# Turning one norm by DMA, moving two feed-forward blocks forward, and letting VectorE take shared-port work

## The chip, the cores and the metric

The kernel runs on one core of a Trainium2 chip. A core has five engines that run side by side: TensorE (PE in the profile, with its weight loads as PEld), VectorE (DVE), ScalarE (ACT), GpSimd (POOL) and SyncE (SP), whose queue issues all DMA transfers here. The metric is the device time of one execution in microseconds, as a median over runs.

## The reference

One transformer block over 2048 rows of 512 features, with shifts, scales and gates from a condition vector `c`:

```python
mod = (_silu(c) @ w_mod).reshape(c.shape[0], 6, 1, -1)
sa, ca, ga, sb, cb, gb = (mod[:, i] for i in range(6))
h = _layernorm(x) * (1 + ca) + sa
x = x + ga * A(h)     # attention: 32 heads of 128, the last 512 rows of the k and v caches
h = _layernorm(x) * (1 + cb) + sb
x = x + gb * B(h)     # (gelu(h @ w_gate) * (h @ w_up)) @ w_down, inner size 1376
```

## The kernel before

Numbers that go through PE are kept as two fp16 parts, a high one and a low one; a product is three matmuls (high with high, high with low, low with high). Making the two parts is a constant need: ACT copies to the high part (`nc.scalar.activation(..., AF.Copy)`), and a subtraction makes the low part. The helper `tt` writes such a subtraction or sum once, as an operation that POOL or DVE may do.

**Stages.** An opening computes the condition's products, norms the rows and prepares the first heads. The attention stage makes 128 steps, each one head for one block of 512 rows (`slot`): query product, scores, exponentials, DMA transposes of the probabilities, product with v, product with wo, added to `acc`. From head pair `WINO` on, query products of four steps are shared by a seven-product scheme over 2 x 2 blocks (`w_product`; sums of inputs go through POOL). While it runs, the largest absolute value of each weight tile is found (`h_max`, four tiles side by side in `mx`); once for each head pair and kind, `h_send` writes the 128 x 4 maxima to DRAM, and `spread_max` reads them back to every partition, reduces them and makes the scale and its inverse.

The feed-forward stage works on two pairs of row blocks: pair 0 is rows 0 to 1023, pair 1 the rest. A unit `(p, f)` is pair p with column block f of 128 of the inner size. It uses the same seven products (`product`), for which the weight parts of block f are made once (`aw_make`: scaling, four sums, six splits) and, for some blocks, shared by both pairs. `UNITS` is the order of the units, `SPLIT` those that make their own parts, `MAKE` which parts are made ahead of which unit. The norm of the second pair (row blocks 2 and 3) hangs on units (0, 2) and (0, 3) of that list through `P1`; its sums on unit (0, 4).

The second norm of one row block is: statistics (`ln2_stats`), four tiles normed in fp32 (`ln2_norm`), four chunks, each turned by four fp32 transposes on PE into a PSUM bank and then scaled and shifted (`ln2_chunk`), and its high and low parts (`ln2_high`, `ln2_low`).

**What sets the order.** Nothing is issued as written. Class `Weaver` records every operation with its cost and dependences, plays the program several times with priorities worked back from the end, and issues what it found; its `Port` is why nearly every row of the profile has line L444. Its costs for each engine stand in `cost`. An operation may be recorded for two engines (`either`), and `sooner` decides in the play which takes it: the one that would end first. POOL and an operation on DVE that reads two SBUF tensors are marked `lock`: the play never lets them overlap. In `sooner`, such an operation on DVE is charged `SHY`, 1500 ns, on top of its cost. Where POOL follows DVE closely, `issue` makes POOL wait for that DVE operation. Any change in the program draws the whole order anew.

## Time and profile before

| | |
|---|---|
| Median of 3 runs | 1657.21 us (1657.04 to 1657.3) |
| Profiled execution | 1657.58 us, its span 1655.8 us |
| Mean granted PE clock | 0.997 |
| Busy: PE, DVE, ACT, POOL | 1642.4, 1289.3, 1216.6, 1305.0 us |
| Matmuls | 7732 |
| DMA | 228.61 MB, 138 GB/s on average |

Busy time is the union of an engine's instructions. For PE the ends are modelled: an instruction's duration includes its way out of the array, while the next one may already have started, so a pace is read from starts. In a row of a timeline, a name such as `psQ<-ident,T` gives the tile that is written and those that are read: `ps...` are PSUM banks, `psS` scores, `pp` probabilities in two parts, `st` row statistics, `raw` loaded weights, `top`, `iv` and `av` a crossing's maximum, scale and inverse, `aw` weight parts of the feed-forward stage, `hid` its inner activations, and `B`, `T` block inputs in two parts.

### The profile page before, as it was taken

How to read it: one execution, taken by the hardware profiler on the slowest of the kernel's cores; microseconds unless marked ns; L12 is line 12 of the kernel's file. 1: busy time of each engine (PE TensorE's matmuls, PEld its weight loads, DVE VectorE, ACT ScalarE, POOL GpSimd, SP SyncE). 2: the span in 40 equal slices, each digit the busy share in tenths (PEclk: the TensorE clock that was granted, in tenths of full speed). 3: DMA queues.
4: the chain of work that ended last, by engine and by line, in shares of the span. 5: the costliest groups of instructions: out<-in, count | busy, mean ns of one | idle time of the engine just before them, and what ended most of it. 6: DMA issues, size and time to landing. Idle time of an engine off the chain costs nothing.

```text
span 1655.8 us, 24293 instructions
## 1 busy us (share of the span) xinstructions
PE 1642.4 (99%) x7732; PEld 764.5 (46%) x7732; DVE 1289.3 (78%) x2381; ACT 1216.6 (73%) x2418; POOL 1305.0 (79%) x1097
## 2 busy tenths in 40 slices
PE   8999999999999999999999999999999999999999
PEld 4444444444444444444444444444444444444455
DVE  7777787878787788788999887888887956656557
ACT  5987797777787777888778777787878876545451
POOL 5999986868586878787768889999977898784682
PEclk9999999999999999999999999999999999999999
DMA  7676697878787778999999997788877712101111
GB/s 241 128 144 130 135 157 143 152 138 149 144 143 140 153 136 157 186 196 194 196 200 205 189 167 148 147 175 179 168 129 158 144 28 64 42 25 51 42 45 52
DMA packets 686289, 228.61 MB, mean 138 GB/s; under 512 B 596432, under 2 KB 663056, under 8 KB 686160
## 3 DMA queue, kind: packets, MB, share of 16 engines
q1 hardware_dynamic: 686160, 227.05, 69.1%
q8 instruction: 61, 1.00, 0.3%
q14 instruction: 68, 0.56, 0.1%
HBM read 78.98 MB, written 5.38 MB: 51 GB/s over the span
## 4 chain that ended last, share of the span: by engine, by line
PE 91%; ACT 2%; POOL 2%; DVE 2%; DMA 1%; SPq 1%; issue 1%; DVEq 0%; POOLq 0%; ACTq 0%
PE psS L444 31%; PE psW L444 23%; PE psO L444 21%; PE psQ L444 17%; SPq L444 1%; DVE st L444 1%; DVE acc L444 1%; DMA pT<-pp 1%; ACT p L444 0%; POOL pp L444 0%; POOL B L444 0%; DMA wm<-in_w_mod_dram 0%; POOL aw L444 0%; ACT T L444 0%; DMA raw<-in_B_w_up_dram 0%
## 5 line engine op out<-in xcount | busy, mean ns | idle before, releaser
L444 POOL TENSOR_TENSOR pp<-p,pp 128x1024 f16<-128x1024 f32 x256 | 545.9, 2132 | 212.8 <-ACT pp L444 97.3
L444 ACT ACTIVATE p<-psS,st,es 128x512 f32<-128x512 f32 x512 | 393.4, 774 | 187.7 <-DVE st L444 186.8
L444 DVE SCALAR_TENSOR_TENSOR acc<-psW,st,acc 128x512 f32<-128x512 f32 x496 | 367.2, 742 | 79.8 <-PE psW L444 77.7
L444 PE MATMUL psW<-wo,oT 128*128 128x512 f16 x1536 | 416.3, 379 | 0.0
L444 PE MATMUL psS<-kT,q 128*128 128x512 f16 x1536 | 379.1, 379 | 2.0 <-ACT q L444 2.0
L444 PE MATMUL psO<-pT,v 128*128 128x512 f16 x1536 | 377.1, 379 | 0.3 <-DMA pT<-pp 0.2
L444 DVE TENSOR_REDUCE st<-psS 128x2 f32<-128x1024 f32 x256 | 312.5, 1221 | 60.0 <-PE psS L444 59.6
L444 ACT ACTIVATE pp<-p 128x1024 f16<-128x1024 f32 x256 | 271.0, 1059 | 3.7
L444 PEld LDWEIGHTS <-q 128*128 128x128 f16 x1536 | 149.9, 98 | 182.1 <-ACT q L444 2.6
L444 PEld LDWEIGHTS <-v 128*128 128x128 f16 x1536 | 150.0, 98 | 181.3 <-DMA pT<-pp 1.2
L444 PEld LDWEIGHTS <-oT 128*128 128x128 f16 x1536 | 150.2, 98 | 180.1 <-DVE oT L444 0.5
L444 PEld LDWEIGHTS <-aw 128*128 128x128 f16 (+1 forms) x840 | 84.2, 100 | 95.1 <-issue 2.0
L444 ACT ACTIVATE oT<-psO 128x512 f16<-128x512 f32 x128 | 76.1, 594 | 66.2 <-PE psO L444 66.1
L444 PE MATMUL psQ<-T,S 128*128 128x512 f16 x504 | 123.3, 379 | 0.0
L444 PE MATMUL psQ<-B,A 128*128 128x512 f16 x480 | 119.6, 381 | 0.1
L444 PE MATMUL psS<-T,aw 128*128 128x512 f16 (+1 forms) x480 | 116.9, 379 | 0.0
L444 DVE SCALAR_TENSOR_TENSOR oT<-psO,oT 128x512 f16<-128x512 f32 x128 | 88.0, 688 | 30.9 <-ACT oT L444 30.6
L444 PEld LDWEIGHTS <-A 128*128 128x128 f16 x696 | 68.3, 98 | 83.3 <-issue 2.3
L444 PEld LDWEIGHTS <-S 128*128 128x128 f16 x672 | 65.8, 98 | 79.3
L444 ACT ACTIVATION_READ_ACCUMULATOR p<-psS,st,es 128x1 f32 x512 | 101.0, 197 | 0.0
L444 POOL TENSOR_TENSOR q<-h,q 128x512 f16<-128x512 f32 x84 | 97.5, 1161 | 2.0 <-ACT q L444 1.8
L444 DVE TENSOR_REDUCE mx<-raw 128x1 f32<-128x512 f32 x128 | 84.2, 674 | 15.6 <-DMA raw<-in_A_wq_dram 9.1
(211 smaller groups left out, 2295.6 us busy)
## 6 DMA issues: line engine op xcount, KB each, us to landing
raw<-in_A_k_cache_dram SPq DMA_DIRECT2D x32, 256.0 KB, 3.9
raw<-in_A_wq_dram SPq DMA_DIRECT2D x32, 256.0 KB, 3.7
raw<-in_A_v_cache_dram SPq DMA_DIRECT2D x32, 256.0 KB, 3.3
raw<-in_A_wo_dram SPq DMA_DIRECT2D x32, 256.0 KB, 3.2
pT<-pp SPq DMA_TRANSPOSE x512, 3.3
sa<-most SPq DMA_DIRECT2D x29, 256.0 KB, 3.8
raw<-in_B_w_gate_dram SPq DMA_DIRECT2D x24, 256.0 KB, 3.1
raw<-in_B_w_up_dram SPq DMA_DIRECT2D x24, 256.0 KB, 3.4
```

The costliest lines, as they stand in the source:

```text
L444: made[n] = real(*a, **k)
```

## The change

There are four edits.

1. The charge `SHY` on a DVE operation that shares POOL's port holds only for operations recorded before `calm`. `calm` is set where the feed-forward code begins in the text; at that point only the opening has been recorded, because the attention stage's operations are recorded by the loop over `slot` further below.
2. The second norm of row blocks 2 and 3 is turned by DMA. `turned_norm` norms a tile with a scale of `HS` folded in, splits it into high and low fp16 parts, `turned` sends both through DMA transposes, and `turned_chunk` joins them again with scale and shift in two operations (one more on DVE). The 32 fp32 transposes on PE go.
3. Units (0, 8) and (0, 9) come ahead of the second pair's first unit, which is now (1, 8); blocks 8 and 9 share weight parts between the pairs, and (1, 6) and (1, 7) make their own, so `SPLIT` has 18 units for 16.
4. In a crossing the maxima are written to DRAM by kind, so that the reduction reads neighbours; the scaling after it moves from DVE to POOL.

```diff
-            mine = max(t, shared[e] if kinds[e][1] else 0.0) + kinds[e][0] + (e == "DVE" and kinds[e][1]) * self.SHY
+            mine = ... + (e == "DVE" and kinds[e][1]) * (self.SHY if n < self.calm else 0.0)
...
+            if big:
+                nc.gpsimd.tensor_scalar(RS[key], RS[key], HS, 1.0, op0=OP.mult, op1=OP.mult)
...
-        t = DG[which[0]] = dram.tile([P, 4], F32, name="most", tag="most", bufs=3)
-        nc.sync.dma_start(t, m[:, 0:4])
+        t = DG[which[0]] = dram.tile([4, P], F32, name="most", tag="most", bufs=3)
+        nc.sync.dma_start(t.rearrange("a p -> p a"), m[:, 0:4])
...
-        nc.vector.tensor_reduce(r, w.rearrange("p (k a) -> p a k", a=4), op=OP.max, axis=AX.X)
+        nc.vector.tensor_reduce(r, w.rearrange("p (a k) -> p a k", a=4), op=OP.max, axis=AX.X)
...
-        nc.vector.tensor_scalar(iv[:, 0:4], r, 1e-30, ROUND / top, op0=OP.max, op1=OP.mult)
+        nc.gpsimd.tensor_scalar(iv[:, 0:4], r, 1e-30, ROUND / top, op0=OP.max, op1=OP.mult)
...
+    nc.calm = len(nc.ops)
...
+    TURNED = (2, 3)
+
+    def turned_norm(qg, j):
+        if j % 2 == 0:
+            t = b_tile(0, N2TAG[qg][j // 2], (P, 2, 2, 2, N // 2))
+            N2[qg, j], N2[qg, j + 1] = t[:, 0], t[:, 1]
+            RT["norm"] = right.tile([P, 2, N], F32, name="hf", tag="p32", bufs=2)
+        n, t = RT["norm"][:, j % 2, :], N2[qg, j]
+        nc.either((S_, V), lambda o: ln_norm(("2", qg), n, acc[4 * qg + j], j, o))
+        n = n.rearrange("p (a n) -> p a n", a=2)
+        nc.scalar.activation(t[:, :, 0, :], n, AF.Copy)
+        tt(t[:, :, 1, :], n, t[:, :, 0, :], OP.subtract)
+
+    def turned(qg, j):
+        for half in range(2):
+            nm = (("B11", "B21"), ("T4", "B22"))[qg % 2][half]
+            d = ff_b(qg // 2, nm).rearrange("p a c n -> p (a c) n")
+            nc.sync.dma_start_transpose(d[:, :, j * P:(j + 1) * P], N2[qg, j][:, half].rearrange("p a n -> p (a n)"))
+
+    def turned_chunk(qg, c):
...
+        a, b = ffs[:, 9 + c:10 + c], colB[2][:, c:c + 1]
+        hi, lo = f_view(qg, c)
+        affine(full, lo, a, b)
+        nc.vector.scalar_tensor_tensor(full, hi, a, full, op0=OP.mult, op1=OP.add)
...
-    UNITS = [(0, f) for f in range(PLAIN, 8)] + [(1, 6), (1, 7)] + [(p, f) for f in range(8, NF - 1) for p in range(2)] + \
-        [(0, NF - 1)] + [(1, f) for f in range(6)] + [(1, NF - 1)]
-    MAKE = {(0, 7): None, (1, 7): 7, (0, 8): 8, (0, 9): 9, (0, 10): 10}
-    SPLIT = [u for u in UNITS if not (u[0] and 6 <= u[1] < NF - 1)]
+    UNITS = [(0, f) for f in range(PLAIN, NF - 1)] + [(1, NF - 3), (1, NF - 2), (0, NF - 1), (1, 6), (1, 7)] + \
+        [(1, f) for f in range(6)] + [(1, NF - 1)]
+    MAKE = {(0, 9): None, (1, 9): 9}
+    SPLIT = [u for u in UNITS if not (u[0] and NF - 3 <= u[1] < NF - 1)]
...
-          [(ln2_norm, 2, j) for j in range(4)] + [(chunk2, 2, c) for c in range(4)],
+          [(g, 2, j) for j in range(4) for g in (turned_norm, turned)] + [(chunk2, 2, c) for c in range(4)],
```

`chunk2` calls `turned_chunk` in place of `ln2_chunk`, and unit (0, 3) has the same new entries for block 3.

**What moves in the attention stage.** POOL, around the low part of one query, the tile `q` made from the fp32 tile `h_580` (`pp<-p_...` are the subtractions for the probabilities of one half step, numbered alike in both programs). Before:

```order
L444 TENSOR_TENSOR pp<-p_629,pp 128x2x512
L444 TENSOR_TENSOR q<-h_593,q 128x512
L444 TENSOR_TENSOR raw<-raw 128x256
L444 TENSOR_TENSOR A_635<-raw,A_635 128x256
L444 TENSOR_TENSOR pp<-p_642,pp 128x2x512
L444 TENSOR_TENSOR q<-h_580,q 128x512
L444 TENSOR_TENSOR S_634<-raw,S_634 128x256
L444 TENSOR_TENSOR k_666<-raw,k_666 128x512
L444 TENSOR_TENSOR pp<-p_652,pp 128x2x512
```

And now:

```order
L444 TENSOR_TENSOR pp<-p_629,pp 128x2x512
L444 TENSOR_TENSOR q<-h_593,q 128x512
L444 TENSOR_TENSOR pp<-p_642,pp 128x2x512
L444 TENSOR_TENSOR pp<-p_652,pp 128x2x512
L444 TENSOR_TENSOR pp<-p_663,pp 128x2x512
L444 TENSOR_SCALAR iv<-top 128x4
```

Between three subtractions for probabilities nothing is left, and a crossing's scaling has come to POOL. The query's low part is now on DVE, between the maxima of the scores (`st<-psS`). DVE before, and behind it DVE now, from the operation that makes `h_580`:

```order
L444 SCALAR_TENSOR_TENSOR h_580<-psQ,h_580 128x512
L444 RECIPROCAL st<-st 128x4
L444 SCALAR_TENSOR_TENSOR acc<-psW,st,acc 128x512
L444 TENSOR_REDUCE st<-psS 128x2
L444 SCALAR_TENSOR_TENSOR acc<-psW,st,acc 128x512
```

```order
L444 SCALAR_TENSOR_TENSOR h_580<-psQ,h_580 128x512
L444 TENSOR_REDUCE mx_80<-raw 128x1
L444 TENSOR_REDUCE st<-psS 128x2
L444 SCALAR_TENSOR_TENSOR acc<-psW,st,acc 128x512
L444 TENSOR_SCALAR st<-st,es 128x1 x2
L444 TENSOR_TENSOR q<-h_580,q 128x512
L444 SCALAR_TENSOR_TENSOR acc<-psW,st,acc 128x512
L444 TENSOR_REDUCE st<-psS 128x2
```

One more operation with two SBUF inputs stands between two score maxima on DVE.

**What moves in the feed-forward stage.** PE before, where the transposes of row block 3's norm (tiles `T_0_3084` and `T_0_3085`) stand among a unit's products:

```order
L444 MATMUL psS<-B_1_2999,aw 128x512
L444 MATMUL psQ<-ident,T_0_3084 128x128
L444 LDWEIGHTS aw
L444 MATMUL psS<-B_1_2999,aw 128x512
L444 LDWEIGHTS aw
L444 MATMUL psS<-T_1_2993,aw 128x512
L444 MATMUL psQ<-ident,T_0_3084 128x128
```

SP's queue now, where row block 2's tiles (`T_0_3045`, `T_0_3049`) are turned into the block inputs `B_0_3047` and `B_0_3048`, between loads of weights:

```order
L444 DMA_TRANSPOSE B_0_3047<-T_0_3045 128x4x128
L444 DMA raw<-in_B_w_down_dram 128x512
L444 DMA_TRANSPOSE B_0_3047<-T_0_3045 128x4x128
L444 DMA raw<-in_B_w_gate_dram 128x4x128
L444 DMA raw<-in_B_w_up_dram 128x4x128
L444 DMA_TRANSPOSE B_0_3048<-T_0_3045 128x4x128 x2
L444 DMA_TRANSPOSE B_0_3047<-T_0_3049 128x4x128
L444 DMA_TRANSPOSE B_0_3048<-T_0_3049 128x4x128
```

PE has no transpose for row blocks 2 and 3 any more; SP's queue has 16 transposes more and four loads of weights more.

More of the change, by code (lines that the diff above doesn't have):

```diff
@@ L1285, in ff_scalars @@
             nc.vector.reciprocal(ffs[:, 8:9], ab)
+            nc.vector.tensor_scalar_mul(ffs[:, 9:13], cols[:, 8:12], ffs[:, 8:9])
             nc.vector.tensor_scalar(cols[:, 8:16], cols[:, 8:16], ffs[:, 8:9], HS, op0=OP.mult, op1=OP.mult)
@@ L1360, in ln2_stats @@
     def ln2_stats(qg, j):
-        ln_stats(("2", qg), acc[4 * qg + j], j)
+        ln_stats(("2", qg), acc[4 * qg + j], j, qg in TURNED)
+    TURNED = (2, 3)
[15 more added lines that the diff above has]
+    def turned_chunk(qg, c):
+        if c % 2 == 0:
+            RT["full"] = right.tile([P, 2, N], F32, name="hf", tag="p32", bufs=2)
+        full = FULL[qg, c] = RT["full"][:, c % 2, :]
+        a, b = ffs[:, 9 + c:10 + c], colB[2][:, c:c + 1]
+        hi, lo = f_view(qg, c)
+        affine(full, lo, a, b)
+        nc.vector.scalar_tensor_tensor(full, hi, a, full, op0=OP.mult, op1=OP.add)
     def ln2_norm(qg, j):
@@ L1817, in chunk2 @@
     def chunk2(qg, c):
-        ln2_chunk(qg, c)
+        turned_chunk(qg, c)
         ln2_high(qg, c)
```

9 lines of the change are left out of this document (5 added, 4 removed).

## The prediction

> **What bounds the kernel now.** I read the page's engine totals first, then the clock row and the chain of waits, then busy time by stretches, and last single rows where the change works.
>
> ```profile
> span 1655.8 us, 24293 instructions
> PE 1642.4 (99%) x7732; PEld 764.5 (46%) x7732; DVE 1289.3 (78%) x2381; ACT 1216.6 (73%) x2418; POOL 1305.0 (79%) x1097
> PEclk9999999999999999999999999999999999999999
> PE 91%; ACT 2%; POOL 2%; DVE 2%; DMA 1%; SPq 1%; issue 1%; DVEq 0%; POOLq 0%; ACTq 0%
> ```
>
> PE is busy for 99% of the span at nearly the full granted clock, and 91% of the chain that ended last is PE. A busy PE need not be a full one, so I look at its pace. The next rows are from busy time by stretches (busy us and count for PE, PEld, DVE, ACT, POOL; then clock, DMA share, GB/s): the opening 60 us, the two fullest stretches for DVE, the crossing into the feed-forward stage, that stage, and the sum line of sixteen stretches that cover 40 to 1310 us.
>
> ```profile
> 0.00:60.00 60.00, 52.42 (x250) 29.63 (x251) 44.16 (x109) 40.65 (x73) 39.70 (x58) 0.94 0.74 206
> 760.00:840.00 80.00, 80.00 (x372) 36.14 (x371) 71.81 (x136) 62.95 (x128) 62.27 (x48) 1.00 1.02 195
> 840.00:920.00 80.00, 79.89 (x371) 36.08 (x370) 72.76 (x140) 61.39 (x124) 60.90 (x46) 1.00 1.02 201
> 1310.00:1345.00 35.00, 34.76 (x177) 17.66 (x176) 30.06 (x54) 29.78 (x55) 31.59 (x34) 1.00 0.47 103
> 1345.00:1650.00 305.00, 303.68 (x1503) 149.58 (x1503) 186.25 (x261) 160.80 (x302) 212.80 (x241) 1.00 0.13 39
> sum 1270.00, PE 1268.61 PEld 576.50 DVE 1041.29 ACT 1005.27 POOL 1040.38; mean PE 79.29 PEld 36.03 DVE 65.08 ACT 62.83 POOL 65.02
> 1239.92 1.29 PE psQ L444 x6
> ```
>
> The last row, from the chain, has six 512-column matmuls in 1.29 us, 0.215 each. A stretch of 80 us holds 371 or 372 of them: 80 / 0.215 = 372. So through the attention stage PE takes one matmul after the other with no hole at all. Idle PE time exists in two places only: 60.00 - 52.42 = 7.6 us in the opening, and about 1.5 us here and there in the feed-forward stage. The time is therefore PE's work plus those holes, and every other engine matters only if it opens a new hole.
>
> **The transposes that leave PE.** The 32 fp32 transposes of the second pair's second norm (two blocks, four chunks of four) are gone from PE. What one costs:
>
> ```profile
> L444 PE MATMUL psQ<-ident,T 128*128 128x128 f32 x32 | 5.6, 276 | 0.0
> 1320.49 0.60 PE L444 MATMUL psQ<-ident,T 128*128 128x128 f32 x4
> 1320.93 1.03 PE L444 MATMUL psO<-pT,v 128*128 128x512 f16 x4
> ```
>
> The first row is the group in 1345 to 1500 us: just these 32, busy 5.6 us. The other two are neighbours on the timeline: four transposes start at 1320.49 and the next matmul at 1320.93, 0.44 us for four, 0.11 each. The 276 ns are mostly the way out of the array, which the next matmul overlaps. So the saving is 32 x 0.11 = 3.5 us, at most the 5.6 us of the busy row; I take 3.5, since the PE's next start is what the chain counts. Each stood among matmuls that run back to back, so nothing hides it.
>
> What replaces them: per tile of 128 rows one norm (as before), a high copy on ACT and a low subtraction, then two DMA transposes; per chunk one more multiply-add on DVE. That is 8 x 2 + 8 = 24 extra vector operations of 0.6 to 1.2 us, some 19 us over ACT, DVE and POOL, and 16 transposes on SP's queue. The 1345 to 1650 row has ACT idle for 144 us, DVE for 119, and a DMA share of 0.13. The existing transposes show what one costs:
>
> ```profile
> pT<-pp SPq DMA_TRANSPOSE x512, 3.3
> ```
>
> It lands 3.3 us after issue. A unit is 42 product matmuls and, on average, 24 for its way down, at 0.215 each 14 us of PE; five units lie between the one that makes the second pair's sums and the pair's first product, so some 70 us cover the whole chain. Costed at nothing; uncovered it would be 3.3 us once per block.
>
> **The reordered units.** Two more first-pair blocks come first, so the second pair's sums get two units more, but blocks 6 and 7 of the second pair now make their own weight parts: two more sets of loads, scales, sums and splits.
>
> ```profile
> L444 POOL TENSOR_TENSOR aw<-raw,aw 128x512 f16<-128x512 f32 x14 | 17.2, 1232 | 23.3 <-ACT aw L444 14.9 <-DVE r L444 7.5 <-ACT r L444 0.9
> L444 POOL TENSOR_TENSOR S1f<-raw 128x256 f32<-128x256 f32 x14 | 11.9, 851 | 3.3 <-issue 1.3 <-ACT r L444 1.2 <-POOL aw L444 0.7
> ```
>
> One split of 512 and five of 256 columns and four sums near the second row's 0.85 us or less are about 8 us of POOL a set, 16 in all, against 92 us that POOL idles in the 1345 to 1650 row. PE's work is unchanged: the products are the same ones in another order. The wait that this order can remove is seen on PE:
>
> ```profile
> 1345.35 0.59 PE L444 MATMUL psS<-B,B 128*128 128x512 f16 x2 [0.60 <-POOL B L444]
> 1462.95 1.46 PE L444 MATMUL psS<-B,aw 128*128 128x512 f16 x6 [0.39 <-DVE r L444]
> 1467.51 0.81 PE L444 MATMUL psS<-B,aw 128*128 128x512 f16 x3 [0.52 <-ACT r L444]
> ```
>
> The last two holes lie where the second pair's first blocks start, behind POOL's sums; together with the first they make 1.5 us. I take half of it, -0.8; the bounds are -1.5 and, if the crossing gets tighter, +2.
>
> **The work that changes engine.** This is the largest edit, though its words don't say so. The planner charged DVE 1.5 us extra for an operation that reads two SBUF tensors. The charge now holds only for operations recorded before the main loop, so 204 subtractions and sums of the attention stage (156 of 512 columns, 48 of 256; I counted them in the two orders) and some 85 of the feed-forward stage go from POOL to DVE. What they cost there:
>
> ```profile
> L444 POOL TENSOR_TENSOR q<-h,q 128x512 f16<-128x512 f32 x84 | 97.5, 1161 | 2.0 <-ACT q L444 1.8 <-DVE st L444 0.2
> L444 POOL TENSOR_TENSOR pp<-p,pp 128x1024 f16<-128x1024 f32 x256 | 545.9, 2132 | 212.8 <-ACT pp L444 97.3 <-issue 91.9 <-DVE acc L444 4.5
> L444 DVE TENSOR_TENSOR r<-psS,h x60: 676/691/693, 1358.0 to 1635.0; 128x512 f32<-128x512 f32 x54, 96x512 f32<-96x512 f32 x6
> L444 DVE TENSOR_TENSOR hid<-r,hid x36: 675/692/1534, 1340.6 to 1643.3; 128x512 f16<-128x512 f32 x32, 96x512 f16<-96x512 f32 x4
> L444 DVE TENSOR_TENSOR hid<-r,hid 128x512 f16<-128x512 f32 x32 | 28.3, 897 | 4.3 <-ACT hid L444 4.1
> L444 DVE TENSOR_REDUCE mff<-raw 128x1 f32<-128x352 f32 x8 | 4.1, 510 | 0.4 <-DMA raw<-in_B_w_up_dram 0.4
> ```
>
> With one operand in PSUM the operation never leaves 676 to 693 ns; with both in SBUF, as all the moved ones have, the least is the same but the mean is 897 and the longest 1534. That surplus of 0.2 us is time spent waiting for POOL. For 256 columns I take 0.41, an estimate from the last row's 510 ns for 352 at the 1.05 ns a column that 512 in 0.68 gives. In the attention stage that is 156 x 0.69 + 48 x 0.41 = 127 us, with the surplus 168. DVE also loses work:
>
> ```profile
> L444 DVE TENSOR_REDUCE top<-sa 128x4 f32<-128x512 f32 x29 | 31.6, 1089 | 7.3 <-DMA sa<-most 7.2
> L444 DVE TENSOR_REDUCE mx<-raw 128x1 f32<-128x512 f32 x128 | 84.2, 674 | 15.6 <-DMA raw<-in_A_wq_dram 9.1 <-DMA raw<-in_A_k_cache_dram 4.8 <-POOL raw L444 1.1
> L444 DVE TENSOR_SCALAR iv<-top 128x4 f32<-128x4 f32 x29 | 6.1, 211 | 0.0
> most<-mx SPq DMA_DIRECT2D x28, 2.0 KB, 1.9
> ```
>
> With the maxima stored by kind, each reduction reads neighbours instead of every fourth value: 1089 should fall to the 674 of the plain reduction, and the 0.21 us scaling goes to POOL: 29 x 0.62 = 18 us less. The scattered 2 KB write becomes 512 pieces for 128; it may land later than 1.9 us, and POOL may hold the scaling for one 2.13 us subtraction, but both lie before a weight scaling that is planned half blocks ahead. Bounds: 0 and, if a scaling comes late, +1.
>
> So DVE goes from 1041 to 1041 + 168 - 18 = 1191 of 1270 us in the attention stage: 94%, still under the stage. POOL drops by 204 operations, near 210 us. No hole follows from the totals; I take +0.3 us and keep 0 and +8 for the range (the price is worked out below). In the feed-forward stage 186 + 85 x 0.9 + 6 = 269 of 305.
>
> **The opening.** The whole order is planned anew. In the first 60 us the maxima of the first weights cross before the modulation columns, two norms move to DVE, and four transposes no longer stand between the first query's products. The first product's lows are still six POOL subtractions of 1.16 us in a row. I find gains and losses near 1 us each and take 0, bounds -2 and +2.
>
> **The sum.** -3.5 - 0.8 + 0.3 + 0 = -4.0 us on the profiled span of 1655.8, so 1651.8. That execution took 1657.58 us, 1.8 more than its span, and lies 0.4 above the median of 1657.21. Against the median: 1653.2 us.
>
> **Rivals.** DVE becomes the bound (slower). Where: 760 to 920 us, where the two rows leave DVE 8.19 + 7.24 = 15.4 us. Some 17 moved operations fall there (those between DVE's 144th and 176th score maxima in the new order), less about 2.5 us for four cheaper crossings. It decides once a moved operation costs more than (15.4 + 2.5) / 17 = 1.05 us on average; at the longest seen, 1.53, the overrun is 26 - 2.5 - 15.4 = 8 us, and PE, whose score banks are released through DVE's maxima, waits for it: 1653.2 + 8 = 1661. For it: the attention stage runs POOL's 2.13 us subtractions between them, longer than what the 897 mean was measured beside. Against: POOL is emptier, and 897 is under 1050. Were every moved operation to sit out a whole 2.13 us subtraction, the 204 would take 204 x 2.82 = 575 us against some 229 idle; the 1.53 maximum speaks against that, so I give it no chance of its own, but it lifts this rival's from one in ten to 0.17. The Trainium skill (SBUF — State Buffer, section "Who interferes with whom") says just that of two such instructions whichever starts second waits for all of the first.
>
> The gain is lost: the new order opens holes of 3 to 4 us in the opening or at 1310 to 1345, where DVE is busy for 30.06 of 35 us and PE's attention work runs out. Then 1657. For it: each of the three holes quoted above lies at such a change of stage. Against: the holes of the whole 305 us after it come to 1.3.
>
> More is gained: transposes at the 5.6 us bound, all 1.5 us of holes gone and 1 us from the opening: 1657.2 - 8.1 = 1649.1.
>
> **How the numbers follow.** Forecast 1653.2 with its own range 1651 to 1655.5: 0.52. More gained: 0.14. Gain lost, 1655.5 to 1660.5: 0.17. DVE the bound: 0.17. A measurement of this kernel tells 0.2% from no change, 3.3 us: below 1653.9 is faster, above 1660.5 slower. Of the forecast's 0.52, 0.38 lies below 1653.9, so faster 0.52, same 0.14 + 0.17 = 0.31, slower 0.17. Leaving out a twentieth below and half of the slower case and a little more above gives 1649.5 to 1661.
>
> **What would show it.** PE must have 32 instructions fewer and still 371 or 372 per 80 us between 40 and 1310 us; a stretch with fewer, ended by DVE or by ACT behind a DVE maximum, is the first rival. The moved subtractions should read 0.69 to 0.9 us on DVE, the maxima's reduction near 0.67. The holes at 1463 and 1467 should be gone. The opening's PE busy time tells its share. I am wrong if DVE passes 97% in a stretch of attention, or if the opening differs by more than 2 us.

## The result

The changed kernel takes 1809.93 us (1802.96 to 1820.5), the kernel before 1656.98 us in the same session: a ratio of 1.0926, 95% interval 1.0893 to 1.0959. It is 153 us slower, where 1653.2 us was forecast and the range ended at 1661. The ratios below leave out one execution, of the kernel with the norm, the units and the late moves: it took 6200.98 us, and why isn't known.

The page of the changed kernel: span, busy time by engine, the granted clock in 40 slices, and the chain that ended last by engine.

```profile
span 1808.5 us, 24455 instructions
PE 1686.5 (93%) x7700; PEld 771.6 (43%) x7700; DVE 1446.3 (80%) x2651; ACT 1227.1 (68%) x2431; POOL 1046.9 (58%) x877
PEclk9999999999999999999999898999899999999999
PE 64%; DMA 15%; DVE 11%; ACT 3%; SPq 3%; issue 2%; POOL 2%; POOLq 0%; ACTq 0%; DVEq 0%
```

PE has the 32 instructions fewer, and DVE's share is 80%, so no engine is full. PE's part of the chain fell from 91 to 64%, and DMA's rose from 1 to 15%. Busy time by stretches of the changed kernel (busy us and count for PE, PEld, DVE, ACT, POOL; then clock, DMA share, GB/s) tells where the time went:

```profile
0.00:60.00 60.00, 51.65 (x251) 31.58 (x252) 48.56 (x118) 41.63 (x77) 32.47 (x51) 0.94 0.77 205
40.00:1310.00 1270.00, 1164.84 (x5203) 517.50 (x5201) 1014.87 (x1909) 887.74 (x1783) 755.09 (x549) 0.96 0.84 143
760.00:840.00 80.00, 73.52 (x333) 32.77 (x332) 67.70 (x128) 56.22 (x116) 39.37 (x29) 0.98 0.82 151
840.00:920.00 80.00, 74.05 (x336) 33.06 (x334) 65.61 (x124) 54.97 (x111) 45.87 (x34) 0.96 0.88 163
1400.00:1520.00 120.00, 119.56 (x570) 56.20 (x569) 107.56 (x195) 92.64 (x178) 81.16 (x76) 1.00 0.60 119
```

Between 40 and 1310 us PE stood idle for 1270 - 1164.84 = 105.2 us, where it had been idle for 1.4; an 80 us stretch holds 333 or 336 matmuls in place of 372. The opening has 8.4 us of idle PE time for 7.6 before, and the stretch from 1400 us on, into which the end of attention now reaches, has 0.4 for 1.0. So the loss lies in the attention stage. It has two parts: over the span PE's idle time grew from 1655.8 - 1642.4 = 13.4 to 1808.5 - 1686.5 = 122.0 us, which is 108.6 us, and its busy time grew by 44.1 us for less work. The granted clock in the second row is 0.96, and a matmul there takes 1164.84 / 5203 = 0.224 us of busy time against 0.215: 0.215 / 0.96 = 0.224. The clock fell behind the longer holes. Two stretches of the changed kernel show it, the first at a hole that ends at 556.63 us after 5.68 us, the second around one of 1.46 us:

```profile
556.00:560.00 4.00, 3.37 (x9) 1.21 (x9) 3.88 (x7) 2.60 (x5) 1.94 (x1) 0.57 0.90 169
617.00:622.00 5.00, 3.79 (x18) 1.79 (x19) 3.60 (x7) 1.71 (x5) 1.42 (x1) 1.00 0.91 172
```

Behind the long hole the granted clock is 0.57 for 4 us; around the short one it stays at 1.00.

Four rows of who waits for whom, in the changed kernel (us in total, times, longest), then the groups and DMA issues of the crossing (the last number of an issue is the median us to its landing):

```profile
DVE top L444 <- DMA sa<-most: 93.9, 19, 8.8
POOL iv L444 <- DVE top L444: 83.3, 17, 10.2
PE psW L444 <- DVE acc L444: 60.9, 19, 7.2
PE psO L444 <- DMA pT<-pp: 25.0, 9, 6.3
...
L444 DVE TENSOR_REDUCE top<-sa 128x4 f32<-128x512 f32 x29 | 19.8, 683 | 93.9 <-DMA sa<-most 93.9
...
sa<-most SPq DMA_DIRECT2D x29, 256.0 KB, 4.9
most<-mx SPq DMA_DIRECT2D x28, 2.0 KB, 9.4
```

The reduction itself is as cheap as forecast (683 ns for 1089). But the write of 2 KB that feeds it lands 9.4 us after its issue, where it had landed after 1.9, and DVE waits 93.9 us for the value in place of 7.2. One crossing on the timeline (start, us, engine, operation, and the idle time before it with its releaser), one engine after another:

```profile
538.89 0.53 SPq L444 DMA_DIRECT2D most<-mx  x1
547.89 0.34 SPq L444 DMA_DIRECT2D sa<-most  x1
...
546.05 0.68 DVE L444 SCALAR_TENSOR_TENSOR oT<-psO,oT 128x512 f16<-128x512 f32 x1
554.72 0.69 DVE L444 TENSOR_REDUCE top<-sa 128x4 f32<-128x512 f32 x1 [7.99 <-DMA sa<-most]
...
555.50 0.23 POOL L444 TENSOR_SCALAR iv<-top 128x4 f32<-128x4 f32 x1 [9.39 <-DVE st L444]
...
555.53 0.30 ACT L444 ACTIVATE st<-st,es 128x4 f32<-128x4 f32 x1 [6.66 <-DVE st L444]
...
556.63 1.01 PE L444 MATMUL psW<-wo,oT 128*128 128x512 f16 x2 [5.68 <-DVE acc L444]
```

SP issues the write at 538.89 and can issue the reading, which waits for it, only at 547.89. DVE comes to the reduction at 546.73 and stands until 554.72. Its next evacuation of a bank stands behind that, and so PE waits 5.68 us; POOL, with the scaling at the head of its line, does nothing for 9.39 us, and ACT nothing for 6.66.

### The profile page after: what moved, and what is told of

It is laid out like the page before. It is cut to its first block, busy times and chain, and to the rows that moved or that the text cites. A ratio compares the mean times of both kernels' runs of the same rounds, so it can differ in the third digit from the quotient of the medians.

```text
span 1808.5 us, 24455 instructions
## 1 busy us (share of the span) xinstructions
PE 1686.5 (93%) x7700; PEld 771.6 (43%) x7700; DVE 1446.3 (80%) x2651; ACT 1227.1 (68%) x2431; POOL 1046.9 (58%) x877
## 4 chain that ended last, share of the span: by engine, by line
PE 64%; DMA 15%; DVE 11%; ACT 3%; SPq 3%; issue 2%; POOL 2%; POOLq 0%; ACTq 0%; DVEq 0%
PE psS L444 23%; PE psW L444 16%; PE psO L444 14%; PE psQ L444 11%; DMA most<-mx 5%; DMA sa<-most 4%; DVE st L444 3%; SPq L444 3%; DVE acc L444 3%; DMA pT<-pp 2%; ACT p L444 1%; POOL pp L444 1%; DVE mx L444 1%; DMA raw<-in_A_wq_dram 1%; DVE h L444 1%
## 5 line engine op out<-in xcount | busy, mean ns | idle before, releaser
L444 PE MATMUL psW<-wo,oT 128*128 128x512 f16 x1536 | 481.0, 387 | 60.8 <-DVE acc L444 60.7
L444 PE MATMUL psO<-pT,v 128*128 128x512 f16 x1536 | 434.4, 385 | 31.7 <-DMA pT<-pp 25.0
L444 PE MATMUL psS<-kT,q 128*128 128x512 f16 x1536 | 435.4, 388 | 1.7 <-ACT q L444 0.8
L444 PE MATMUL psQ<-T,S 128*128 128x512 f16 x504 | 147.6, 391 | 11.4 <-DVE q L444 10.9
L444 PE MATMUL psQ<-B,A 128*128 128x512 f16 x480 | 137.2, 390 | 4.1 <-DVE h L444 3.4
L444 DVE TENSOR_REDUCE top<-sa 128x4 f32<-128x512 f32 x29 | 19.8, 683 | 93.9 <-DMA sa<-most 93.9
```

The source lines that it names most:

```text
L444: made[n] = real(*a, **k)
```

## The experiments

Each run has a run of the kernel before beside it; in these its median lay between 1656.71 and 1657.48 us.

**Is it the write?** Two kernels exchange only the stored layout, and the order of all instructions on PE, DVE, ACT and POOL stays that of the kernel they start from. The first is the changed kernel with the layout of before:

```diff
-        t = DG[which[0]] = dram.tile([4, P], F32, name="most", tag="most", bufs=3)
-        nc.sync.dma_start(t.rearrange("a p -> p a"), m[:, 0:4])
+        t = DG[which[0]] = dram.tile([P, 4], F32, name="most", tag="most", bufs=3)
+        nc.sync.dma_start(t, m[:, 0:4])
-        nc.sync.dma_start(w, t.rearrange("a p -> (a p)").partition_broadcast(P))
+        nc.sync.dma_start(w, t.rearrange("p a -> (p a)").partition_broadcast(P))
-        nc.vector.tensor_reduce(r, w.rearrange("p (a k) -> p a k", a=4), op=OP.max, axis=AX.X)
+        nc.vector.tensor_reduce(r, w.rearrange("p (k a) -> p a k", a=4), op=OP.max, axis=AX.X)
```

> The changed kernel with one thing undone: the four maxima of a row are written side by side again (128 pieces of 16 bytes) and the reduction reads every fourth value. The scaling stays on POOL, and all instructions of PE, DVE, ACT and POOL stand in the same order as in the changed kernel. Theory L (the loss is the landing of the scattered write): the write lands 1.9 us after its issue as before, the reduction waits for its transfer some 7 us in all instead of 94, PE has 371 or 372 matmuls per 80 us of attention again, and the time is that of the prediction's other terms, 1651 to 1657 us. Rival D (the 204 operations that moved to DVE, or the scaling on POOL behind two-operand subtractions, hold PE up): the write is fast and the time stays above 1780 us; DVE's reductions show waits on other things than the transfer.

It took 1662.84 us, ratio 1.003 (1.002 to 1.0041). Its stretches, its reduction and its write:

```profile
0.00:60.00 60.00, 49.87 (x247) 29.43 (x248) 47.87 (x117) 40.91 (x76) 32.04 (x50) 0.94 0.75 203
40.00:1310.00 1270.00, 1262.72 (x5856) 573.08 (x5855) 1148.04 (x2150) 992.96 (x1999) 841.23 (x612) 1.00 0.83 158
...
L444 DVE TENSOR_REDUCE top<-sa 128x4 f32<-128x512 f32 x29 | 31.5, 1086 | 14.3 <-DMA sa<-most 14.3
...
most<-mx SPq DMA_DIRECT2D x28, 2.0 KB, 2.4
```

Four lines take back 147 of the 153 us, though the 204 moved operations and the scaling on POOL are still in place. Theory L holds and rival D falls. But the reduction waits 14.3 us, twice what was expected, and 5.4 us over the kernel before are left (its ten runs lie between 1657.33 and 1666.1 us), where 4 under it were expected; that is taken up below. The second is the kernel before with the layout of the change, the same four lines the other way round:

> The kernel before with the stored layout of the crossings alone: by kind, 512 pieces of 4 bytes, and the reduction over neighbours. Nothing else is changed, and PE, DVE, ACT and POOL keep the order of before. Theory L: the landing goes from 1.9 to about 9 us here too; 28 crossings lose what exceeds their slack. In the changed kernel that was 153 us / 28 = 5.5 us each, so 1657 + 100 to 160 = 1757 to 1817 us. Rival S (only the new order, which fills DVE to nine tenths in attention and puts the scaling on POOL, has no slack for a late landing): below 1690 us, though the write is as late. Rival D: 1657 us or less, by the cheaper reduction.

1783.53 us, ratio 1.0758 (1.074 to 1.0776): the layout alone costs 126 us, within what theory L gave. The write lands after 9.3 us, and DVE's reduction waits 120.6 us for its reading. Rival S falls: the order of before has no slack for this either.

**Late value, or held transfers?** The planner orders each engine by how long it thinks things take. In the next run it knows that the write lands 7.5 us later.

```diff
-                end = bus + 650.0
+                end = bus + 650.0 + 7500.0 * (n in self.sent)
```

(with the same 7500 in its two passes on urgency; `sent` holds the writes to the device memory).

> The changed kernel whose planner is told that a write to the device memory lands 7.5 us later than it thought (in its play of the order, and in its two passes that work out how urgent each operation is). The program is the same, its order on every engine is drawn anew. Theory L in the form L1 (only the standing still in line costs: DVE's reduction comes to the head of its queue before the value is there, and everything behind it waits): the planner now puts some 7 us of other work ahead, the reduction's wait falls from 94 us to under 25, and the time to 1655 to 1675 us. Form L2 (the transfers queued behind the write are held up too, above all the transposes of the probabilities that PE waits for): the reduction's wait falls, but PE still waits for transposed probabilities, 1690 to 1760 us. Rival D: 1780 us or more.

1759.37 us, ratio 1.0615 (1.06 to 1.0631). The planner did its part, and it was not enough. Waits of this kernel, then SP's queue around one write:

```profile
PE psW L446 <- DVE acc L446: 32.9, 13, 6.1
PE psO L446 <- DMA pT<-pp: 31.5, 14, 3.8
DVE mx L446 <- DMA raw<-in_A_wq_dram: 29.5, 9, 8.8
DVE top L446 <- DMA sa<-most: 12.9, 9, 4.1
...
526.45 0.51 SPq L446 DMA_DIRECT2D most<-mx  x1
527.01 0.53 SPq L446 DMA_DIRECT2D ga<-msum  x1
529.41 9.32 SPq L446 DMA_TRANSPOSE pT<-pp  x2
538.83 0.53 SPq L446 DMA_DIRECT2D raw<-in_A_v_cache_dram  x1
```

The reduction's wait is down from 93.9 to 12.9 us, yet 102 of the 153 us stay. Now it is transposed probabilities and loads of weights that come late: two transposes that follow the write take SP 9.32 us. In the kernel before, an issue takes (ns; least, median, longest):

```profile
L444 SPq DMA_TRANSPOSE pT<-pp x512: 1231/1326/4018, 42.7 to 1320.1; - x171
```

The longest is 4.0 us there and 10.6 in the changed kernel. That is form L2: the write holds up what is issued behind it. A direct test adds such a write where nobody reads it, to the kernel before, right behind each reading of the maxima:

```diff
+    unread = nc.nc.dram_tensor("unread", [128, P], F32, kind="Internal").ap()
+    nc.extra = lambda port, i: port.dma_start(unread[4 * i:4 * i + 4].rearrange("a p -> p a"), ones[:, 0:4])
             made[n] = real(*a, **k)
+            if n in self.sent:
+                self.extra(self.nc.sync, self.sent.index(n))
```

> The kernel before, unchanged but for 29 extra writes: right behind each reading of the maxima SP issues a scattered write of 512 4-byte pieces of a constant to a place in the device memory that nobody reads. No value is late; layout and order of all other work are those of before. Theory Q (the write holds up the transfers issued behind it, so that transposes and loads land up to 10 us late): PE waits for transposed probabilities, and most of the 102 us that stayed when the planner knew of the late value comes back: 1720 to 1780 us. Theory V (only the late value costs): 29 more issues on SP of about 0.5 us, 1657 to 1662 us.

1744.3 us, ratio 1.0524 (1.0508 to 1.0539): 87 us, 3.0 for each of the 29 unread writes. Theory Q holds. Its DMA issues and three of its waits:

```profile
unread<-ones SPq DMA_DIRECT2D x29, 2.0 KB, 9.2
most<-mx SPq DMA_DIRECT2D x28, 2.0 KB, 2.1
...
DVE top L444 <- DMA sa<-most: 46.0, 14, 6.6
PE psO L444 <- DMA pT<-pp: 27.2, 10, 5.8
PE psW L444 <- DVE acc L444: 26.3, 14, 4.0
```

One thing in the expectation was not so: it said that no value is late, but the reading of the maxima, whose data were still under way, was caught by the write issued behind it: 10 of the 29 readings landed after 6.0 us or more, where the longest took 5.2 in the kernel before, and DVE waited 46.0 us in place of 7.2. The hold reaches transfers on both sides of the write, and PE's 26.3 us behind DVE belong to the caught readings at least in part, so the 87 us aren't the price of the transfers behind the write alone. The same writes, issued by ACT:

```diff
-                self.extra(self.nc.sync, self.sent.index(n))
+                self.extra(self.nc.scalar, self.sent.index(n))
```

> The same 29 unread scattered writes, issued by ACT in place of SP. If the hold is in the queue on which the write was issued, SP's transfers are free of it, and the time is 1657 to 1668 us, the cost of ACT's own issues. If the hold is in what all queues share, it is within 15 us of the run with the writes on SP's queue.

1829.83 us, ratio 1.1038 (1.1016 to 1.106), worse than on SP's queue and not within the 15 us named. The reading in the kernel before, then the DMA issues of this kernel, and its first crossing on the timeline:

```profile
sa<-most SPq DMA_DIRECT2D x29, 256.0 KB, 3.8
...
sa<-most SPq DMA_DIRECT2D x29, 256.0 KB, 10.4
unread<-ones ACTq DMA_DIRECT2D x29, 2.0 KB, 11.0
...
154.34 0.38 ACTq L1896 DMA_DIRECT2D unread<-ones  x1
155.26 0.34 SPq L444 DMA_DIRECT2D sa<-most  x1
```

The reading of the maxima on SP's queue lands after 10.4 us instead of 3.8. So another queue is no way out: what is held is shared by both. The Trainium skill (DMA: Bandwidth & Descriptors, section "Issuing engines are not separate DMA queues") says that transfers run on the same 16 DMA engines whichever engine starts them, and interleave there; this run agrees. The reading suffers more than with SP's writes, and the order of issue has changed: ACT issues the write before SP issues the reading at all 29 crossings, by 0.3 to 5.1 us. So here the reading always stands behind the write, where before the write stood behind the reading.

**Number of pieces, or their size?** First the changed kernel with two of a row's four maxima side by side: 256 pieces of 8 bytes.

```diff
-        t = DG[which[0]] = dram.tile([4, P], F32, name="most", tag="most", bufs=3)
-        nc.sync.dma_start(t.rearrange("a p -> p a"), m[:, 0:4])
+        t = DG[which[0]] = dram.tile([2, P, 2], F32, name="most", tag="most", bufs=3)
+        nc.sync.dma_start(t.rearrange("b p a -> p b a"), m[:, 0:4].rearrange("p (b a) -> p b a", b=2))
...
```

(The reading and the reduction follow the layout, and one line of the planner keeps its order as it was.)

> The changed kernel with the maxima written in two halves instead of by kind: two of a row side by side, so 256 pieces of 8 bytes instead of 512 of 4; the reduction reads every second value. Order of PE, DVE, ACT and POOL as in the changed kernel. Theory L with the landing set by the count of pieces: 1.9 us + (9.4 - 1.9) x (256 - 128) / (512 - 128) = 4.4 us; of the 2.5 us more than before, about 2 lie in the slack that 7.5 - 5.5 shows, so 28 x 0.5 = 14 us over the layout of before, near 1667 us (bounds 1652 and 1725, the latter without any slack). Theory L with the landing set by the small size of a piece, whatever the count: it lands after 8 us or more, above 1770 us. Rival D: 1780 us or more.

1668.63 us, ratio 1.0061 (1.0041 to 1.0081), at a landing of 3.6 us, near what the count of pieces gave (4.4 us and 1667). The next keeps the pieces of 4 bytes and writes them as four transfers of 128:

```diff
-            made[n] = real(*a, **k)
+            made[n] = real(*a, **k) if n not in self.sent else [real(a[0][:, i:i + 1], a[1][:, i:i + 1]) for i in range(4)][-1]
```

> The changed kernel with the same bytes written to the same places in the same 4-byte pieces, but as four transfers of 128 pieces, one for each kind, in place of one of 512. The planner doesn't know, and the order on PE, DVE, ACT and POOL is that of the changed kernel. If the number of pieces in one transfer sets the landing (128 pieces 1.9 to 2.4 us, 256 pieces 3.6, 512 pieces 9.4): each lands 2 to 3 us after its issue, the last some 4 us after the first was issued (three more issues of 0.53 us), and the time is near that of 256 pieces, 1662 to 1685 us. If the size of a piece sets it: the last still lands 8 us or more after the first issue, and the time stays at 1780 us or more.

1805.03 us, ratio 1.0887 (1.0871 to 1.0903): no change worth the name, and the count's forecast of 1662 to 1685 falls. But 512 pieces were under way at once here too, so the run does not settle it. Three more do, with unread writes of other shapes in place of the 512 pieces of 4 bytes, again behind each reading; the lines are those of the first, the second and the third (the shape of `unread` changes with them):

```diff
-    port.dma_start(unread[4 * i:4 * i + 4].rearrange("a p -> p a"), ones[:, 0:4])
+    port.dma_start(unread[i].rearrange("a p -> p a"), ones[:, 0:1])
+    port.dma_start(unread[i].rearrange("a p -> p a"), ones[:, 0:2])
+    port.dma_start(unread[i].rearrange("a p c -> p a c"), ones[:, 0:8].rearrange("p (a c) -> p a c", c=2))
```

> The kernel before with an unread write of 128 pieces of 4 bytes behind each reading of the maxima. If the count of pieces sets the hold: it lands like the 128 pieces of 16 bytes, about 2 us after its issue, and the time is 1657 to 1660 us. If the 4-byte size does (about 9.2 us / 512 = 18 ns a piece with an offset, or a fixed price): it lands after 4 us or more, and the time is 1662 us or above.

> The same with 256 pieces of 4 bytes. Count: it lands like the 256 pieces of 8 bytes, 3.6 us after its issue, 1657 to 1668 us. Size: later than those, 5 us or more, and above 1675 us.

> The same with 512 pieces of 8 bytes, twice the data of the scattered write. Count: it lands like 512 pieces of 4 bytes, about 9.2 us after its issue, and the time is near the 1744 us of those, 1730 to 1760. Size: it lands clearly earlier, 7 us or less (twice the 3.6 us of 256 pieces of 8 bytes), and the time is under 1715 us.

The DMA issue of each, in that order:

```profile
unread<-ones SPq DMA_DIRECT2D x29, 0.5 KB, 8.2
```

```profile
unread<-ones SPq DMA_DIRECT2D x29, 1.0 KB, 8.5
```

```profile
unread<-ones SPq DMA_DIRECT2D x29, 4.0 KB, 6.1
```

| pieces of the unread write | landing, us | kernel, us | ratio and interval | loss for each write, us |
|---|---|---|---|---|
| 128 of 4 bytes | 8.2 | 1695.54 | 1.0235 (1.0217 to 1.0253) | 1.3 |
| 256 of 4 bytes | 8.5 | 1709.34 | 1.0316 (1.0295 to 1.0337) | 1.8 |
| 512 of 4 bytes | 9.2 | 1744.3 | 1.0524 (1.0508 to 1.0539) | 3.0 |
| 512 of 8 bytes | 6.1 | 1677.58 | 1.012 (1.0099 to 1.0142) | 0.7 |

It is the size that makes the landing late. A quarter of the pieces of 4 bytes lands hardly sooner (8.2 us for 9.2), while twice the data in pieces of 8 bytes lands 3 us earlier and costs a quarter. What the kernel loses grows with the count as well. All four writes stand behind a reading that itself lands after a median of 3.9 to 4.3 us, so their landings compare with each other, and not with the 1.9 us of the crossing's own write. Counted from the landing of that reading, the median is 4.9, 5.1 and 5.4 us for 128, 256 and 512 pieces of 4 bytes, and 1.5 us for 512 of 8. The run with 128 pieces also shows the hold on the transfers behind the write with little else: 2 of the 29 readings are caught (DVE waits 14.7 us for them), and still 39 us are lost, with PE waiting 19.0 us for transposed probabilities. What in the memory or the DMA engines makes 4 bytes so dear, no run shows; nor was it tried whether such pieces would be as dear if they didn't lie next to each other in the memory. The same page of the Trainium skill (section "Specifications") names 512 bytes as the size below which a write turns into a read and a write; here all shapes lie below it, and 512 pieces of 8 bytes land after 6.1 us and 512 of 4 bytes after 9.2, so that line doesn't part the cheap ones from the dear.

**The rest of the change.** With the fast write the kernel still takes 1662.8 us, 9.6 over the forecast. Four runs take the rest apart; all have the layout of before, and in all the planner draws the whole order anew. First the charge for the whole program:

```diff
-    nc.calm = len(nc.ops)
+    nc.calm = 1 << 30
```

> The changed kernel with the four maxima side by side again (the fast write, 1662.8 us so far) and the planner's charge of 1.5 us kept for the whole program, so that the two-operand subtractions and sums stay on POOL. The turned norm, the order of the units and the scaling on POOL remain. Theory A (the 9.6 us between 1662.8 and the predicted 1653.2 are DVE's load: late score maxima and evacuations open holes of 0.5 to 2.3 us on PE): DVE's busy time falls to about 1290 us, and the time to 1652 to 1655 us. Theory B (the moves are harmless; the scaling on POOL, behind POOL's long subtractions, or the order drawn anew makes the holes): it stays at 1658 us or above.

Then the kernel before with the limited charge and nothing else of the change:

```diff
-(e == "DVE" and kinds[e][1]) * self.SHY
+(e == "DVE" and kinds[e][1]) * (self.SHY if n < self.calm else 0.0)
...
+    nc.calm = len(nc.ops)
```

> The kernel before with one edit: the planner's charge holds only for operations recorded ahead of the main loop, so some 290 two-operand operations go from POOL to DVE; layout, scaling, norm and units as before. Theory A: DVE's busy time rises from 1289 to about 1460 us, PE gets holes in the attention stage, and the time is 1661 to 1668 us. Theory B: 1655 to 1659 us.

Then the changed kernel with another engine for the scaling:

```diff
-        nc.gpsimd.tensor_scalar(iv[:, 0:4], r, 1e-30, ROUND / top, op0=OP.max, op1=OP.mult)
+        nc.vector.tensor_scalar(iv[:, 0:4], r, 1e-30, ROUND / top, op0=OP.max, op1=OP.mult)
```

> The changed kernel with the four maxima side by side again and the scaling of the maxima back on DVE; turned norm, units and the planner's limited charge remain. Theory A: the scaling is not the cause, 1660 to 1665 us. Theory B in the form that POOL's scaling, which waits in line behind subtractions of 2.13 us, delays the weights: 1655 us or less.

And the edits of the first and the third together:

> Of the change only the second pair's turned norm and the order of the units: maxima side by side, scaling on DVE, the planner's charge for the whole program. Theory A: the two terms of the prediction that speak of PE's work alone, -3.5 and -0.8 us, so 1652 to 1654 us. Theory B: the order drawn anew gives holes of its own, 1656 us or above. If DMA transposes in the feed-forward stage cost more than thought, PE waits for them there.

They took 1668.89 (1.0063 to 1.0087), 1670.38 (1.0066 to 1.009), 1660.9 (1.0008 to 1.0029) and 1664.7 us (1.0033 to 1.0057). The third came out within the range of theory A, and the second went its way and 2 us past its range; the first and last did not: taking the moves back made it slower. The stretches in the table below show why: without the moves the holes in the attention stage shrink (to 5.8 and 1.7 us) and others open in the feed-forward stage. So two kernels keep the charge in the attention stage only; they differ in the scaling, on DVE and on POOL:

```diff
-    nc.calm = len(nc.ops)
     SLOTS = ("q", "q", "q", "k16", "A1", "A1", "raw2", "raw2")
...
     assert not bg, bg
+    nc.calm = len(nc.ops)
     plain_act((0, 1))
```

> The changed kernel with the maxima side by side, the scaling on DVE, and the planner's charge kept for everything recorded up to the end of the attention slots; it is dropped only for what is recorded after them (the feed-forward stage). The turned norm and the new unit order stay. Theory P (two engines bound two stages: with the charge POOL is late in the feed-forward stage, 12.2 us of PE holes between 1400 and 1550 us; without it DVE is late in attention, 6 to 13 us of holes): attention as in the kernel with the charge throughout (0 to 2 us of holes), feed-forward as in the kernel without it (under 2 us), so 1664.7 - 12.2 + 1 = 1653.5 us, 1651 to 1656. Rival O (any order drawn anew loses some 5 to 10 us somewhere, wherever the charge holds): 1660 us or above.

> The same with the scaling of the maxima on POOL, as in the changed kernel. Theory P: 1652 to 1657 us; the scaling changes the order more than the work. Rival O: 1660 us or above, and the holes lie in other places than in the run beside it.

And the norm and the units were tried each alone. For the norm, the kernel with both gets the units of before; for the units, the kernel before gets the lines marked + in the change's own diff:

```diff
-    UNITS = [(0, f) for f in range(PLAIN, NF - 1)] + [(1, NF - 3), (1, NF - 2), (0, NF - 1), (1, 6), (1, 7)] + \
-        [(1, f) for f in range(6)] + [(1, NF - 1)]
-    MAKE = {(0, 9): None, (1, 9): 9}
+    UNITS = [(0, f) for f in range(PLAIN, 8)] + [(1, 6), (1, 7)] + [(p, f) for f in range(8, NF - 1) for p in range(2)] + \
+        [(0, NF - 1)] + [(1, f) for f in range(6)] + [(1, NF - 1)]
+    MAKE = {(0, 7): None, (1, 7): 7, (0, 8): 8, (0, 9): 9, (0, 10): 10}
```

> The kernel before with the second pair's turned norm alone: units, layout, scaling and the charge of before. Theory U (the new unit order makes the feed-forward holes, since it asks POOL for two more sets of weight parts in a stretch where POOL also makes the second pair's sums): no more holes than before, 1657.2 - 3.5 = 1653.7 us, 1652 to 1656. Theory N (the turned norm makes them, with its extra operations and transposes): 1662 us or above.

> The kernel before with the new order of the units and of their weight parts alone. Theory U: the holes of 1400 to 1550 us are there, 1664.7 + 3.5 = 1668 us, 1664 to 1670. Theory N: near the kernel before, 1656 to 1659 us.

PE's idle time by stretch, from busy time by stretches of each kernel, all with the fast write:

| kernel | charge holds in | median, us | ratio and interval | idle 0-60 | idle 40-1310 | idle 1400-1520 |
|---|---|---|---|---|---|---|
| before | all | 1657.2 | 1 | 7.6 | 1.4 | 1.0 |
| turned norm alone | all | 1670.15 | 1.0081 (1.0067 to 1.0095) | 7.2 | 0.8 | 12.5 |
| units alone | all | 1660.31 | 1.0016 (1.0007 to 1.0025) | 7.2 | 5.6 | 0.0 |
| norm, units | all | 1664.7 | 1.0045 (1.0033 to 1.0057) | 7.3 | 1.7 | 7.1 |
| norm, units, scaling on POOL | all | 1668.89 | 1.0075 (1.0063 to 1.0087) | 7.6 | 5.8 | 8.3 |
| moves alone | opening | 1670.38 | 1.0078 (1.0066 to 1.009) | 8.1 | 10.1 | 0.0 |
| norm, units, moves | opening | 1660.9 | 1.0019 (1.0008 to 1.0029) | 8.9 | 7.0 | 0.4 |
| the same, scaling on POOL | opening | 1662.84 | 1.003 (1.002 to 1.0041) | 10.1 | 7.3 | 1.2 |
| norm, units, late moves | attention | 1655.78 | 0.9993 (0.9984 to 1.0002) | 5.8 | 0.9 | 2.0 |
| the same, scaling on POOL | attention | 1655.19 | 0.9987 (0.9978 to 0.9996) | 7.4 | 2.5 | 1.2 |

The turned norm alone came out as theory N said, and theory U falls; the units alone took 1660.31 us, between the ranges of the two, but with no hole between 1400 and 1520 us. The turned norm opens 7 to 12.5 us of holes between 1400 and 1520 us wherever the charge keeps its subtractions on POOL, and none to speak of where they may go to DVE. Theory P holds, and rival O falls: both kernels lie within the ranges that P gave them. Dropping the charge costs 7 to 10 us of holes in attention, against 0.8 to 5.8 with it, and saves them in the feed-forward stage. The redrawn order by itself moves single cells by some 4 us (units alone has 5.6 in attention, norm and units together 1.7), so what the scaling or the units are worth alone stays open. Keeping the charge in attention and dropping it later gives the best two kernels, 1.4 and 2.0 us under the kernel before. The second interval excludes 1, but both lie within the 0.2% that counts as no change here.

Where the turned norm waits, in the kernel with it alone; the timeline of ACT, DVE and PE at the largest hole:

```profile
1435.08 1.52 ACT L444 ACTIVATE hf<-T,cols,ffs 128x512 f32<-128x512 f16 x2 [5.67 <-DMA T<-T]
1435.92 0.75 DVE L444 SCALAR_TENSOR_TENSOR hf<-T,ffs,hf 128x512 f32<-128x512 f16 x1 [5.27 <-ACT hf L444]
1436.59 0.74 DVE L444 SCALAR_TENSOR_TENSOR acc<-psW,ffs,acc 128x512 f32<-128x512 f32 x1
1437.39 2.29 PE L444 MATMUL psW<-wd,hid 128*128 128x512 f16 x5 [3.15 <-DVE acc L444]
```

The low halves are subtracted on POOL, one after the other behind weight sums, then turned by DMA; ACT stands 5.67 us before the turned tile, DVE 5.27 us behind ACT, and the evacuation that PE's bank needs stands behind DVE. It is the crossing's pattern again. Two other holes of this stretch, of 2.35 and 2.16 us, end with ACT's scaling of `wd`, for which ACT had waited for POOL; so POOL is late there for more than the turned tiles. The largest hole in attention shows the pattern too; DVE and PE in the changed kernel with the layout of before:

```profile
822.42 1.06 DVE L444 TENSOR_REDUCE top<-sa 128x4 f32<-128x512 f32 x1 [2.80 <-DMA sa<-most]
823.41 1.22 DVE L444 TENSOR_REDUCE st<-psS 128x2 f32<-128x1024 f32 x1
824.54 1.40 DVE L444 SCALAR_TENSOR_TENSOR acc<-psW,st,acc 128x512 f32<-128x512 f32 x2
...
825.33 0.38 PE L444 MATMUL psW<-wo,oT 128*128 128x512 f16 x1 [2.12 <-DVE acc L444]
```

Of this kernel's eight holes over 0.2 us between 60 and 1310 us, three, with 3.3 of 5.5 us, come within 6 us behind such a wait for a crossing. What began the others isn't shown.

## Why the prediction was wrong

**What bounds the kernel** was read rightly: PE without a hole in attention, so that any new wait in it counts in full. (Its list of holes leaves out some 4 us behind 1650 us; the changed kernel with the layout of before has as much there.)

**The step that failed** is the one on the crossing's write, in the part on the work that changes engine: "The scattered 2 KB write becomes 512 pieces for 128; it may land later than 1.9 us ... but both lie before a weight scaling that is planned half blocks ahead. Bounds: 0 and, if a scaling comes late, +1." Measured: the write lands after 9.4 us, and its layout alone costs 126 us on the kernel before and 147 in the changed one. Three things were wrong in it. The cover of half a block is the cover of the weights, not of DVE: the reduction stands in DVE's line where the planner, which still reckoned with the old landing, had put it, and an engine that waits in line delays everything behind it. The row beside the bound was for another shape (128 pieces of 16 bytes, 1.9 us), and no term was worked out for a late landing itself; 28 crossings by the longest landing of a transpose in the trace before, 6.8 us, less the 1.9, give an estimate of 137 us. That this comes so near the 126 is luck, but its size would have warned. And no thought was given to the transfers beside the write, which carry a large part of the loss: unread writes, behind which no value is late but the readings that they catch, cost 87 us, and 102 stayed when the planner knew of the late value. How the loss divides between the late value and the held transfers no run tells exactly.

**The transposes off PE**, -3.5: PE's busy total went from 1642.4 to 1639.7 us in the kernel with the fast write, and to 1639.3 in the one that keeps the charge in attention. About 3 us, as forecast.

**The turned norm at nothing** was right only by another edit of the same change. The cover of 70 us that the prediction named holds while DVE may take the subtractions; with them on POOL the norm costs 7 to 12.5 us of holes. The price named for lost cover, 3.3 us once per block or 6.6 for both, was too small, as it left out who waits in line behind the turned tile.

**The reordered units**, -0.8: with the units alone PE is full from 1400 to 1520 us, so the holes of 1463 and 1467 do go; in the change with the fast write other holes take their place (118.84 us busy for 119.03 before). The kernel gained nothing from it.

**The moves to DVE**, +0.3 with +8 as bound: the durations were right (47 subtractions `q<-h,q` at 754 ns on DVE, against 690 to 900 forecast; the groups of five and more moved operations of 512 columns have means between 682 and 981, and the longest single one took 2.05 us, where 1.53 was the longest seen before). DVE is busy for 1148 of 1270 us, 90% where 94 were forecast, and in no stretch of 80 us above 95%. The term was mis-sized within its bounds: 1270 - 1262.72 = 7.3 us idle against 1.4, so +5.9, and +8.7 with the moves alone. The rival of DVE as the bound gave 1661, and the kernel with the fast write took 1662.8, but not by that rival's mechanism: it put the whole overrun at 760 to 920 us with DVE full, whereas 2.5 of the 7.3 us lie there, with DVE busy for 92%, and the largest hole starts where DVE waits 2.80 us for the value of a crossing, at 822 us. So the nearness of the two times is luck. The means of the moved groups, at most 981 ns, leave no room for a wait for a whole POOL subtraction (2.13 us) at each of them, a case that the prediction had priced and given no chance of its own. The Trainium skill (SBUF — State Buffer, section "Who interferes with whom") has the instruction that comes second wait for the whole of the first. The trace agrees where the two meet: the longest one starts at 118.83 us, 0.64 us into a POOL subtraction of 2.14 us, and ends 0.54 us behind it; but by the means this is rare.

**The opening**, 0 with bounds of 2 either way: 10.1 us idle for 7.6 in the kernel with the fast write, +2.5, just outside; over all orders drawn it went from 5.8 to 10.1.

## What to carry to other kernels

An engine that runs its instructions in line turns a late value into a stop of everything behind it, so price a slower producer by its landing less the work really placed ahead of its consumer, once per use, and not by when the final result is needed. Don't trade a cheap contiguous write for a cheaper read: 12 us of strided reduction on an engine with spare time were saved, at the price of a write in single 4-byte elements that held up transfers near it. When two edits shift load between engines, look at each stage by itself; a rule that is right in one stage can be wrong in the next.

## What was not expected of the hardware

A write to the device memory in pieces of 4 bytes lands 8.2 us after its issue for 128 pieces and 9.2 for 512, while 512 pieces of 8 bytes take 6.1, all behind a reading of 256 KB; a crossing's own write, with no such reading right ahead, takes 9.4 for 512 of 4 bytes, 3.6 for 256 of 8, and 1.9 to 2.4 for 128 of 16. Such a write holds up transfers around it, also those of SP's queue when ACT issued it (readings of 256 KB from 3.8 to 10.4 us), and SP's issue of the next transposes with it (9.32 us for two, at 1.33 each). And PE's holes cost more than their length: with 105 us of them in 1270 us the granted clock there was 0.96, and a matmul's busy time 4% longer.
